# Block attention feeding a snake MLP: two batches per step, two tokens per partition, attention in one block of 64x64 tiles

## Chip, cores, metric

One core of one Trainium2 chip. The time is the device time of the core in microseconds (us), the median of several executions; a profiled execution gives a "span", about 1.9 us shorter. Lower is better. Some executions of a kernel fall into a slower state with a lower clock (the kernel before: 239.35 us at a clock of 0.986 against 234.49 us at 0.998, on one chip). Ratios and their 95% intervals use runs of the fast state alone; a median is that of all runs. The experiments' rounds ran on six different chips, so kernels of different rounds are compared by their ratios to the kernel before, which ran in every round.

The engines are PE (TensorE; PEld are its weight loads), DVE (VectorE), ACT (ScalarE), POOL (GpSimd) and SP (SyncE). Matmuls write into PSUM, which the kernels use in banks (m_ps, A_ps and Z_ps in the views before, PS in those after).

## The reference, cut to what matters

```python
# q, k, v: (4 batches, 8 heads, 768 tokens, 64), float32; block = 64
for b in range(nb):                                     # linear attention with decay lam[h]
    intra = ((qb @ kb.T) * Dmask) @ vb                  # inside the block, causal
    inter = (qb * lam_pow) @ kv_state                   # from the running state
    out[block] = intra + inter
    kv_state = lam_block * kv_state + (kb * rev_pow).T @ vb
x = out.transpose(0, 2, 1, 3).reshape(3072, 512)        # heads side by side
h = x @ w_in                                            # 512 -> 2048
g = h + sin(alpha * h) ** 2 / (alpha + 1e-9)            # "snake"
y = g @ w_out                                           # 2048 -> 512, float32 out
```

Both kernels work in tokens of 128 and six "chunks" of 512 tokens. Attention is done in 24 "steps". The scaled q and k (a power of lam each) replace the decay mask, so that the state needs no scaling.

## The kernel before

A small recorder takes operations in program order. PE keeps that order; the other engines' operations are ordered once, before the launch, by a simple simulation that uses assumed durations. Each engine then executes its queue strictly in that order (below, DVE stands 6.26 us in front of one operation with finished work queued behind it). A step is one batch, 128 tokens, all 8 heads. A load puts one token into each of 128 partitions, as 8 packets of 256 bytes. In the names, T are the transposes of q and k, S the products of k and q inside a block, O the output (`intra` and `inter` of the reference) and Z the product of k and v that updates the state. xT is the attention's output as the MLP reads it, gT the activation between the MLP's two halves; each half's weights, w_in and w_out, are loaded in blocks.

```python
def load(s):                                   # one step: three DMAs of 256 KB, on SP's queue
    b, n, r = s // NB, s % NB, s % RL
    sl = slice(n * BL, (n + 1) * BL)
    for nme, src, dst in (("k", k, k32), ("q", q, q32), ("v", v, v32)):
        a = src[b, :, sl, :].rearrange("h p d -> p h d")
        rec_load(lambda e, a=a, d=dst[r]: e.dma_start(d[:, :, :], a), ...)

def att_T(s, bank=None):                       # 8 transposes 128x128, then one copy
    for jp in range(HP):
        last = e.transpose(dst[:, jp, :], q2[c][:, 2 * jp:2 * jp + 2, :], ident[:, :])
    ...                                        # the same for k
    rec("DVE", lambda e: e.tensor_copy(qkT[j][:, :, :], dst), 0.7, ...)

def att_S(s):                                  # visit 1: S = k q^T in tiles of 64x128, then the mask
    for jp in range(HP):
        for h in range(2):
            rows = slice(64 * h, 64 * h + 64)
            last = e.matmul(A_ps[:, 4 * h + jp, :], qkT[j][rows, 4 + jp, :], qkT[j][rows, jp, :])
    ...

def att_O(s, bank=None):                       # visit 2: inter 128x128, intra 128x64, Z; then T of the next step
    ...

def grp_A(c, m):                               # MLP in: 4 matmuls 128x512 = one "group"
    ...                                        # PE -> ACT sin -> square (POOL mostly) -> DVE gT
def grp_B(c, s4, m4, bank):                    # MLP out: 4 matmuls = one group
    ...
    if m4 == 3:
        rec("ACT", lambda e: e.copy(osb[o][:, :], m_ps[bank][:, :]), 0.6, ...)
        row0 = TCH * c + 128 * s4
        rec("ACT", lambda e: e.dma_start(out[row0:row0 + 128, :], osb[o][:, :]), 0, ...)
...
for c in range(1, NCH):                        # from chunk 1 on: B of chunk c and A of chunk c + 1 alternate,
    for i in range(NM):                        # with the two attention visits of a step among 8 groups
        grp_B(c, i // 4, i % 4, bank)
        attend(4 * (c + 2), 2 * i, 8, 2, 6, 2)
        grp_A(c + 1, i)
        attend(4 * (c + 2), 2 * i + 1, 8, 2, 6, 2)
```

Of the kernel before, what the change touches and what calls it, by code (L numbers as in the profile page):

```python
# [6 lines left out]
ALU = mybir.AluOpType  # L7
# [7 lines left out]
class Op:  # L15
    __slots__ = ("eng", "fn", "deps", "dur", "idx", "sem_after", "slot", "kslot",
                 "pos", "users", "start", "end", "nbytes", "clock", "prio", "signal", "soft", "soft_users")

    def __init__(self, eng, fn, dur, idx):
        self.eng, self.fn, self.dur, self.idx = eng, fn, dur, idx  # L20
        self.deps = set()
        self.soft = ()
        self.slot = None
        self.kslot = 0
        self.signal = False
        self.prio = idx


class Program:
# [41 lines left out]
    def schedule(self, hop=0.12, rate=270e3, dma_fixed=2.0, issue=0.65):  # L71
# [10 lines left out]
        free = {e: 0.0 for e in self.ENGINES}  # L82
# [9 lines left out]
        while len(order) < n:  # L92
# [26 lines left out]
            if op.slot is not None:  # L119
                free[e] = t + issue  # L120
                dma_free = max(dma_free, t + issue) + op.nbytes / rate
                op.end = dma_free + dma_fixed
            else:
                op.end = t + op.dur
                free[e] = op.end
# [14 lines left out]
    def emit(self, nc, sem):  # L140
# [9 lines left out]
        for op in order:  # L150
            k = known[op.eng]
            need = {}
            for d in op.deps:
                if d.slot is not None:
                    key, val = ("dma", d.slot), d.kslot
                else:
                    if d.eng == op.eng and op.slot is None and d.eng == "PE":
                        continue
                    key, val = d.eng, d.pos
# [48 lines left out]
def bass_lightning_attn__then__act_snake_kernel(  # L208
# [12 lines left out]
    DM = H * D  # L221
# [8 lines left out]
    HP = H // 2  # L230
    RL = 6
    RC = 5
    NPS = 5
    RT = 4
# [4 lines left out]
    with es:  # L239
# [9 lines left out]
        q32 = ring("q32", RL, [128, H, D], F32)  # L249
        k32 = ring("k32", RL, [128, H, D], F32)  # L250
        v32 = ring("v32", RL, [128, H, D], F32)
        q2 = ring("q2", RC, [128, H, D], BF16)
        k2 = ring("k2", RC, [128, H, D], BF16)
        v2 = ring("v2", RC, [128, H, D], BF16)
        qkT = ring("qkT", 2, [128, 8, 128], BF16)
        S_m = ring("S_m", 2, [128, 8, 128], BF16)
        Zs = ring("Zs", 2, [128, HP, 128], BF16)
# [7 lines left out]
        mask = sb("mask", [128, 128], BF16)  # L265
        zeros = sb("zeros", [128, 512], BF16)
        maskf = sb("maskf", [128, 128], F32)
        ident = sb("ident", [128, 128], BF16)
        lam_bc = sb("lam_bc", [128, H], F32)
        E_i = sb("E_i", [128, NB, H], I32)  # L270
        E_f = sb("E_f", [128, NB, H], F32)
        lnlam = sb("lnlam", [128, H], F32)
        lnL = sb("lnL", [128, NB, H], F32)
        Lq = sb("Lq", [128, NB, H], F32)
        Lk = sb("Lk", [128, NB, H], F32)
# [7 lines left out]
        A_ps = es.enter_context(nc.psum_tensor("A_ps", [128, 8, 128], F32))  # L283
        Z_ps = es.enter_context(nc.psum_tensor("Z_ps", [128, HP, D], F32))
        m_ps = [es.enter_context(nc.psum_tensor(f"m_ps_{i}", [128, 512], F32)) for i in range(NPS)]
# [3 lines left out]
        nm_at = [0]  # L289
        last_load = [None]  # L290

        def rec_load(fn, writes, slot, nbytes, after=()):
            soft = (last_load[0],) if last_load[0] is not None else ()
            last_load[0] = rec("SP", fn, 0, writes=writes, slot=slot, nbytes=nbytes, after=after, soft=soft)

        def next_bank():
            i = nm_at[0] % NPS
            nm_at[0] += 1
            return i

        wblk, gate = [], {}
        last_mask = [None]

        def load(s):
            after = [gate[s]] if s in gate else []
            b, n, r = s // NB, s % NB, s % RL
            sl = slice(n * BL, (n + 1) * BL)
            for nme, src, dst in (("k", k, k32), ("q", q, q32), ("v", v, v32)):
                a = src[b, :, sl, :].rearrange("h p d -> p h d")
                rec_load(lambda e, a=a, d=dst[r]: e.dma_start(d[:, :, :], a),  # L310
                         [f"{nme}32.{r}"], f"{nme}{r}", 330000, after)

        def consts():
# [4 lines left out]
            rec("POOL", lambda e: e.iota(E_i[:, :, :], [[128, NB], [0, H]], base=0, channel_multiplier=1), 0.2,  # L318
                writes=["E_i"])
            rec("DVE", lambda e: e.tensor_copy(E_f[:, :, :], E_i[:, :, :]), 0.2, reads=["E_i"], writes=["E_f"])  # L320
            rec("ACT", lambda e: e.activation(lnlam[:, :], lam_bc[:, :], ACTF.Ln), 0.3,
                reads=["lam", "table"], writes=["lnlam"])
            ln_b = bass.AP(lnlam, 0, [[H, 128], [0, NB], [1, H]])
            rec("DVE", lambda e: e.tensor_tensor(lnL[:, :, :], E_f[:, :, :], ln_b, ALU.mult), 0.2,
                reads=["E_f", "lnlam"], writes=["lnL"])
            rec("ACT", lambda e: e.activation(Lq[:, :, :], lnL[:, :, :], ACTF.Exp), 0.3,
                reads=["lnL"], writes=["Lq"])
            rec("ACT", lambda e: e.activation(Lk[:, :, :], lnL[:, :, :], ACTF.Exp, scale=-1.0), 0.3,
# [3 lines left out]
                out=ident[:, :], in_=maskf[:, :], pattern=[[-1, 128]], compare_op=ALU.not_equal, fill=1.0,  # L332
                base=0, channel_multiplier=1), 0.3, reads=["maskf"], writes=["ident"])
            rec("POOL", lambda e: e.affine_select(
                out=mask[:, :], in_=maskf[:, :], pattern=[[-1, 128]], compare_op=ALU.is_gt, fill=1.0,
                base=0, channel_multiplier=1), 0.3, reads=["maskf"], writes=["mask"])
# [3 lines left out]
            for i in range(2):  # L340
                rec("DVE", lambda e, i=i: e.memset(Zs[i][:, :, :], 0.0), 0.3, writes=[f"Zs.{i}"])
# [3 lines left out]
        def alpha_ops():  # L345
            rec("ACT", lambda e: e.dma_start(alpha_r[:, :], moe_alpha.rearrange("(m p) -> m p", p=128)), 0,
                writes=["alpha_r"], slot="alpha", nbytes=8192)
            rec("PE", lambda e: e.transpose(Z_ps[:, 0, 0:NM], alpha_r[:, :], identf[0:NM, 0:NM]), 0.3,
                reads=["alpha_r", "identf"], writes=["Z"])
            rec("ACT", lambda e: e.copy(alpha_sb[:, :], Z_ps[:, 0, 0:NM]), 0.2, reads=["Z"], writes=["alpha"])  # L350
# [4 lines left out]
        def w_block(j, soft=(), after=()):  # L355
            if j < 4:
                cs = slice(512 * j, 512 * (j + 1))
                src = moe_w_in[:, cs].rearrange("(c p) f -> p c f", p=128)
                op = rec("POOL", lambda e: e.dma_start(w1[:, :, cs], src), 0, writes=[f"w1.{j}"],
                    slot=f"w1_{j}", nbytes=700000, soft=soft, after=after)  # L360
            else:
                j2 = j - 4
                src = moe_w_out[512 * j2:512 * (j2 + 1), :].rearrange("(m p) d -> p m d", p=128)
                op = rec("POOL", lambda e: e.dma_start(w2[:, 4 * j2:4 * (j2 + 1), :], src), 0, writes=[f"w2.{j2}"],
                    slot=f"w2_{j2}", nbytes=700000, soft=soft, after=after)
            wblk.append(op)

        def prep(s, fast=False, soft=()):
            n, r, c = s % NB, s % RL, s % RC
            Lq_b = bass.AP(Lq, n * H, [[NB * H, 128], [1, H], [0, D]])  # L370
            Lk_b = bass.AP(Lk, n * H, [[NB * H, 128], [1, H], [0, D]])
            done = rec("POOL", lambda e: e.tensor_tensor(k2[c][:, :, :], k32[r][:, :, :], Lk_b, ALU.mult), 1.05,
                       reads=[f"k32.{r}", "Lk"], writes=[f"k2.{c}"], soft=soft)
            rec("DVE" if fast else "POOL", lambda e: e.tensor_tensor(q2[c][:, :, :], q32[r][:, :, :], Lq_b, ALU.mult),
# [287 lines left out]
```

## Time and profile before

| | before |
|---|---|
| time, median (3 runs) | 234.67 us (234.05 to 237.13) |
| span of the profiled run, granted clock | 232.7 us, 1.000 |
| first MLP matmul | 22.5 us |
| first MLP matmul of chunk 1 | 64.0 us |
| end of the last MLP matmul to the end of the span | about 3 us |
| step period in the steady part | 8.59 us |

The first view is the page of the profiled execution. The rows of digits cut the span into 40 slices: each digit is the busy share in tenths, or for PEclk the clock that TensorE was granted.

```profile
span 232.7 us, 3924 instructions
PE 211.0 (91%) x1571; PEld 105.4 (45%) x1598; DVE 128.4 (55%) x169; ACT 123.2 (53%) x217; POOL 134.1 (58%) x141
...
PE   0687988697999989999999999999999999999994
...
PEclk9999999999999999999999999999999999999999
...
q1 hardware_dynamic: 74880, 18.88, 42.7%
...
q10 hardware_dynamic: 3632, 6.31, 7.4%
...
out_dram<-osb ACTq DMA_DIRECT2D x24, 256.0 KB, 2.0
```

PE is the busiest engine, and its idle time lies in the first third. q1 is SP's queue, the loads; q10 is ACT's queue, the 24 stores of 256 KB. A store lands 2.0 us after its issue. The columns of a queue are packets, megabytes, and the packets' time as a share of 16 DMA engines' span.

The second view gives stretches of the same run: the stretch, its length, busy time of each engine (with its count), the granted clock, the mean busy share of the 16 DMA engines, and GB/s.

```profile
core 0: us, PE busy (x) PEld busy (x) DVE busy (x) ACT busy (x) POOL busy (x), PEclk, DMA share, GB/s
...
4.00:9.00 5.00, 1.69 (x17) 1.29 (x17) 1.74 (x3) 2.76 (x7) 1.83 (x2) 1.00 1.29 228
...
45.00:64.00 19.00, 16.58 (x170) 9.07 (x174) 10.21 (x12) 7.77 (x16) 6.21 (x6) 1.00 1.10 222
...
86.00:216.00 130.00, 129.09 (x899) 63.27 (x913) 69.80 (x92) 72.19 (x124) 83.10 (x82) 1.00 0.34 80
216.00:233.00 17.00, 13.58 (x63) 5.96 (x61) 1.84 (x3) 3.03 (x5) 0.00 (x0) 1.00 0.20 77
```

From 4 to 9 us the loads move 228 GB/s with all DMA engines busy (a share above 1 means that the times of packets on one engine overlap). From 86 to 216 us PE is busy 129.1 of 130 us, so there only less work on PE can gain.

The third view is PE's timeline over one step of the steady part (start, duration, engine, line, operation, output<-inputs, shapes, count).

```profile
170.65 0.81 PE L470 MATMUL m_ps<-xT,w 128*128 128x512 bf16 x3
...
173.98 0.40 PE L410 MATMUL A_ps<-qkT 64*128 64x128 bf16 x8
...
177.78 0.39 PE L430 MATMUL A_ps<-qkT,Zs 128*128 128x128 bf16 x4
178.09 0.41 PE L434 MATMUL A_ps<-S_m,v_2 128*64 128x128 bf16 x8
178.34 0.29 PE L449 MATMUL Z_ps<-v_2,k_2 128*64 128x64 bf16 x8
178.56 0.40 PE L396 MATMUL A_ps<-ident,q_3 128*128 128x128 bf16 x4
178.79 0.39 PE L398 MATMUL A_ps<-ident,k_3 128*128 128x128 bf16 x4
179.23 0.81 PE L470 MATMUL m_ps<-xT,w 128*128 128x512 bf16 x3
```

The group at 170.65 and the one at 179.23 stand at the same place of two steps: the period is 8.58 us. Eight MLP groups take 8 x 0.864 = 6.91 us of it, so the two visits of attention cost about 1.68 us a step.

### The profile page before, as it was taken

To read this page: it belongs to the slowest core of one execution; us is meant where nothing else is said; L and a number is where in the kernel's file an instruction comes from. 1 tells how busy PE (TensorE), PEld (TensorE's weight loads), DVE (VectorE), ACT (ScalarE), POOL (GpSimd) and SP (SyncE) were. 2 spreads that over 40 slices of the span, in tenths; PEclk is the share of its full clock that TensorE was granted. 3 is DMA by queue.
4 is the path that set the end of the run, shared out by engine and by line. 5 is a ranking of instruction groups with operands and counts; after the bars stand their busy time and mean duration, and the time that the engine had idled before them with its cause. 6 is when DMAs were issued, how large, how long until landed. Compare 5 with 4: busy or idle time off the path is not lost.

```text
span 232.7 us, 3924 instructions
## 1 busy us (share of the span) xinstructions
PE 211.0 (91%) x1571; PEld 105.4 (45%) x1598; DVE 128.4 (55%) x169; ACT 123.2 (53%) x217; POOL 134.1 (58%) x141
## 2 busy tenths in 40 slices
PE   0687988697999989999999999999999999999994
PEld 0354433244455544455455455455455444444441
DVE  1664599745668876645636645546556535545300
ACT  4345774032787885655655655575465454454221
POOL 3253789340569897669568568758754554454100
PEclk9999999999999999999999999999999999999999
DMA  6999999999999999999670110111011011101112
GB/s 142 219 182 159 206 195 206 216 207 202 250 294 203 226 215 218 249 223 219 139 180 1 48 45 9 40 45 43 5 45 46 2 45 45 45 3 45 64 71 90
DMA packets 82752, 29.61 MB, mean 127 GB/s; under 512 B 75552, under 2 KB 79664, under 8 KB 82736
## 3 DMA queue, kind: packets, MB, share of 16 engines
q1 hardware_dynamic: 74880, 18.88, 42.7%
q0 software_dynamic: 4224, 4.19, 11.4%
q10 hardware_dynamic: 3632, 6.31, 7.4%
q8 instruction: 12, 0.20, 0.4%
q14 instruction: 4, 0.03, 0.0%
HBM read 27.28 MB, written 6.29 MB: 144 GB/s over the span
## 4 chain that ended last, share of the span: by engine, by line
PE 73%; DVE 8%; DMA 5%; SPq 4%; ACT 3%; issue 2%; POOL 2%; ACTq 0%; POOLq 0%
PE m_ps L498 33%; PE m_ps L470 28%; SPq L310 4%; DVE gT L488 3%; DMA w<-in_moe_w_out_dram 3%; PE A_ps L410 3%; DVE S_m L414 3%; PE A_ps L434 2%; DMA q_3<-in_q_dram 2%; PE A_ps L396 2%; PE A_ps L398 1%; POOL u_1 L486 1%; PE A_ps L430 1%; POOL u_0 L486 1%; ACT xT L443 1%
## 5 line engine op out<-in xcount | busy, mean ns | idle before, releaser
L498 PE MATMUL m_ps<-w,gT 128*128 128x512 bf16 x377 | 94.0, 380 | 2.7 <-DVE gT L488 1.3
L470 PE MATMUL m_ps<-xT,w 128*128 128x512 bf16 x366 | 92.3, 380 | 3.8 <-DVE gT L488 1.7
L498 PEld LDWEIGHTS m_ps<-w,gT 128*128 128x128 bf16 x384 | 36.6, 98 | 46.6 <-DVE gT L488 1.7
L470 PEld LDWEIGHTS m_ps<-xT,w 128*128 128x128 bf16 x384 | 35.2, 98 | 43.0 <-DVE gT L488 3.1
L486 POOL TENSOR_TENSOR u_0<-t_0 128x512 bf16<-128x512 bf16 x24 | 25.1, 1047 | 23.1 <-ACT t_0 L474 23.1
L414 DVE TENSOR_TENSOR S_m<-A_ps,mask 128x1024 bf16<-128x1024 f32 x24 | 29.4, 1223 | 11.7 <-PE A_ps L410 11.0
L488 DVE SCALAR_TENSOR_TENSOR gT<-u_1,r_sb,m_ps 128x512 bf16<-128x512 bf16 x24 | 17.9, 746 | 23.3 <-POOL u_1 L486 23.3
L488 DVE SCALAR_TENSOR_TENSOR gT<-u_3,r_sb,m_ps 128x512 bf16<-128x512 bf16 x24 | 17.9, 744 | 20.7 <-POOL u_3 L486 19.9
L486 POOL TENSOR_TENSOR u_1<-t_1 128x512 bf16<-128x512 bf16 x24 | 24.9, 1038 | 5.1 <-ACT t_1 L474 5.0
L486 POOL TENSOR_TENSOR u_2<-t_2 128x512 bf16<-128x512 bf16 x24 | 24.9, 1039 | 5.1 <-ACT t_2 L474 5.0
L474 ACT ACTIVATE t_2<-m_ps,alpha_sb 128x512 bf16<-128x512 f32 x24 | 16.5, 687 | 19.4 <-PE m_ps L470 19.3
L474 ACT ACTIVATE t_1<-m_ps,alpha_sb 128x512 bf16<-128x512 f32 x24 | 16.5, 687 | 18.1 <-PE m_ps L470 18.1
L486 POOL TENSOR_TENSOR u_3<-t_3 128x512 bf16<-128x512 bf16 x12 | 12.5, 1039 | 23.0 <-ACT t_3 L474 23.0
L474 ACT ACTIVATE t_0<-m_ps,alpha_sb 128x512 bf16<-128x512 f32 x24 | 16.5, 687 | 15.3 <-PE m_ps L470 15.2
L488 DVE SCALAR_TENSOR_TENSOR gT<-u_0,r_sb,m_ps 128x512 bf16<-128x512 bf16 x24 | 17.8, 740 | 10.1 <-POOL u_0 L486 10.1
L488 DVE SCALAR_TENSOR_TENSOR gT<-u_2,r_sb,m_ps 128x512 bf16<-128x512 bf16 x24 | 17.9, 744 | 9.6 <-POOL u_2 L486 9.6
L443 ACT CAST xT<-A_ps 128x512 bf16<-128x512 f32 x20 | 11.6, 582 | 20.9 <-PE A_ps L434 15.4
L506 ACT COPY osb<-m_ps 128x512 f32<-128x512 f32 x24 | 14.1, 586 | 15.6 <-PE m_ps L498 15.5
L474 ACT ACTIVATE t_3<-m_ps,alpha_sb 128x512 bf16<-128x512 f32 x24 | 16.5, 687 | 4.0 <-PE m_ps L470 3.8
L401 DVE COPY qkT<-A_ps 128x1024 bf16<-128x1024 bf16 x20 | 13.7, 684 | 4.7 <-PE A_ps L398 4.7
L457 ACT CAST Zs<-Z_ps 64x256 bf16<-64x256 f32 x40 | 14.6, 366 | 0.6
L410 PE MATMUL A_ps<-qkT 64*128 64x128 bf16 x192 | 10.0, 226 | 2.0 <-DVE qkT L401 1.9
(173 smaller groups left out, 176.8 us busy)
## 6 DMA issues: line engine op xcount, KB each, us to landing
out_dram<-osb ACTq DMA_DIRECT2D x24, 256.0 KB, 2.0
w<-in_moe_w_in_dram POOLq DMA_DIRECT2D x4, 512.0 KB, 8.0
w<-in_moe_w_out_dram POOLq DMA_DIRECT2D x4, 512.0 KB, 6.8
k_0<-in_k_dram SPq DMA_DIRECT2D x4, 256.0 KB, 4.4
q_0<-in_q_dram SPq DMA_DIRECT2D x4, 256.0 KB, 5.1
v_0<-in_v_dram SPq DMA_DIRECT2D x4, 256.0 KB, 5.4
k_1<-in_k_dram SPq DMA_DIRECT2D x4, 256.0 KB, 5.5
q_1<-in_q_dram SPq DMA_DIRECT2D x4, 256.0 KB, 5.8
```

Of the source, the lines that this page charges most:

```text
L310: rec_load(lambda e, a=a, d=dst[r]: e.dma_start(d[:, :, :], a), [f"{nme}32.{r}"], f"{nme}{r}", 330000, after)
L401: rec("DVE", lambda e: e.tensor_copy(qkT[j][:, :, :], dst), 0.7, reads=[key], writes=[f"qkT.{j}"])
L410: last = e.matmul(A_ps[:, 4 * h + jp, :], qkT[j][rows, 4 + jp, :], qkT[j][rows, jp, :])
L414: rec("DVE", lambda e: e.tensor_tensor(S_m[j][:, :, :], A_ps[:, :, :], mask_b, ALU.mult), 1.25, reads=["S0", "S1", "mask"], writes=[f"S_m. ...
L443: rec("ACT", lambda e: e.copy(xT[x][:, :, col:col + 128], dst), 0.62, reads=[key], writes=[f"x.{x}.{s % 4}"])
L457: rec("ACT", lambda e, rows=rows, cols=cols: e.copy(Zs[j][rows, :, cols], Z_ps[rows, :, :]), 0.4, reads=["Z"], writes=[f"Zs.{j}"])
L470: last = e.matmul(m_ps[i][:, :], w1[:, kc, 128 * m:128 * (m + 1)], xT[x][:, kc, :], start=(kc == 0), stop=(kc == NKC - 1))
L474: rec("ACT", lambda e: e.activation(t16[tt][:, :], m_ps[i][:, :], ACTF.Sin, scale=alpha_sb[:, m:m + 1]), 0.7, reads=[f"m.{i}", "alpha"], w ...
L486: return e.tensor_tensor(u16[tt][:, :], t16[tt][:, :], t16[tt][:, :], ALU.mult)
L488: rec("DVE", lambda e: e.scalar_tensor_tensor(out=gT[g][:, m, :], in0=u16[tt][:, :], scalar=r_sb[:, m:m + 1], in1=m_ps[i][:, :], op0=ALU.m ...
L498: last = e.matmul(m_ps[bank][:, :], gT[g][:, m, 128 * s4:128 * (s4 + 1)], w2[:, m, :], start=(m == 0), stop=(m == NM - 1))
L506: rec("ACT", lambda e: e.copy(osb[o][:, :], m_ps[bank][:, :]), 0.6, reads=[f"m.{bank}"], writes=[f"o.{o}"])
```

## The change

Its intent: make attention cheaper on PE and loads cheaper on the DMA engines. A step becomes two batches x 64 partitions, with two neighbouring tokens in each partition and four of the eight heads. A packet becomes 2 tokens x 64 x 4 bytes = 512 bytes. With 64 partitions per batch everything in attention can run in tiles of 64x64, four beside each other, so that transposes, S, intra, inter and Z of three different steps run in one visit. Around that, the order of the stages is new, the MLP's PSUM banks rotate through a list, and the loads of steps 4 to 11 are released by the third w_out block's landing. Because the tokens of a partition are neighbours, the rows that come out of the MLP are permuted, and the store has to put them back.

The core of the diff, with cuts:

```diff
-        for nme, src, dst in (("k", k, k32), ("q", q, q32), ("v", v, v32)):
-            a = src[b, :, sl, :].rearrange("h p d -> p h d")
-            rec_load(lambda e, a=a, d=dst[r]: e.dma_start(d[:, :, :], a), [f"{nme}32.{r}"], ...)
+        for nme in what:
+            for u in range(2):                       # u: which batch of the two
+                off = (((2 * pair + u) * H + HS * hh) * S + n * BL) * D
+                a = bass.AP(src.tensor, off, [[2 * D, 64], [S * D, HS], [1, 2 * D]])
+                op = rec_load(lambda e, a=a, d=dst[r], u=u: e.dma_start(d[half(u), :, :], a), ...)
 ...
-        def att_T(s, bank=None): ...
-        def att_S(s): ...
-        def att_O(s, bank=None): ...
+        def sec(t=None, o=None, s=None, tb=None, sb_=S_BK, ob=O_BK, copy_eng="DVE"):
+            # one visit: transposes of step t, output and state of step o, S of step s
+            ...
+            seqs = [block(first), block(mid), block(second)]   # each spread over four 64x64 tiles
+            ...                        # "second" waits until "first" has retired (a fence)
 ...
-                row0 = TCH * c + 128 * s4
-                rec("ACT", lambda e: e.dma_start(out[row0:row0 + 128, :], osb[o][:, :]), 0, ...)
+                row0 = (2 * pair + u) * S + n * BL
+                dst = bass.AP(out.tensor, row0 * DM, [[DM, 2], [2 * DM, 64], [1, DM]])
+                rec("ACT", lambda e: e.dma_start(dst, osb[o][:, :]), 0, ...)
 ...
-    def schedule(self, hop=0.12, rate=270e3, dma_fixed=2.0, issue=0.65):
+    def schedule(self, hop=0.1, rate=270e3, begin=1.2, done=1.2):
+        issue = {"SP": 0.25, "POOL": 0.8, "ACT": 0.5}
```

## The prediction

> **What bounds the kernel now.** The span is 232.7 us at full clock (cores view). The MLP is 768 matmuls of 128x512 at 0.216 us start to start: 166 us that stay. The chain of waits is 73% PE, with its gaps early.
>
> 1. Head: the first MLP matmul starts at 22.5 us. Until 16.6 us the chain is the load of step 3's q. Loads are 256-byte packets; the trace's take 18 ns (median) on one of 16 engines, about 220 GB/s (windows view: 218).
> 2. Chunk 1's first MLP matmul starts at 64.0 us: of the 41.5 us between, 32 MLP groups are 27.6, four attention steps about 6.6; the rest waits, mostly for the last w_out blocks (6.5 us in the chain) and the S, mask, O round trips.
> 3. Steady state, 86 to 216 us: PE is busy 129.1 of 130 us (windows). A step's period is 8.59 us (starts in the chain); 8 MLP groups are 6.91, so attention costs 1.68: streams of about 1.2 us, and gaps of about 0.1 us around its two visits and between its array shapes (timeline).
>
> **What changes.** Loads become 512-byte packets. The few in the trace take 27 ns, about 300 GB/s (estimate): 2.6 us a step instead of 3.6.[...] Weights start near 12 us instead of 16.4.
>
> Attention becomes one visit per step in 64x64 tiles: 32 transposes, 16 S, 16 intra, 8 inter, 16 Z: at 56 ns per 128 columns and four tiles in parallel, 0.90 us.[...] The trace shows column pairs 4 ns apart every 56 ns; quads it does not show. I add 0.2 for entering and leaving, 0.15 for the fence (the second part waits for the first to retire) and 0.05 for same-tile neighbours: 1.3 us instead of 1.68. On the 16 steps after chunk 1 starts that is 6 us.
>
> **The sum.** First MLP matmul at 16.5 us, partly at half clock (no warm-up matmuls); that hides behind what follows. Weights land until about 36 us. Loads of steps 4 to 7 are gated behind the third w_out block (33 us), so step 7 lands near 46 and chunk 1 starts near 51 (now 64): 13 us gained. After it: 160 MLP groups, 138 us; 17 visits of 1.3, 22; stalls 3 (four PSUM banks in rotation, POOL squares in chunk 1, xT evictions); end 2.5, as now. Span 216.5; timed runs are 1.9 above it: **218.5 us, range 211 to 226**. Faster by over 2%: 0.95; within 2%: 0.04; slower: 0.01.
>
> **What would show it.** Right: near 300 GB/s before 14 us and half the load packets (37,000); first MLP matmul at 15 to 18 us; chunk 1 at 49 to 54; step period 8.1 to 8.3 us; PE still over 97% busy there. Wrong: visits of 1.6 us or more; PE waiting for gT writes, with four banks.
>
> **What would make it wrong.** Dispatch of 176 small PE instructions per visit slower than 5 ns each; a cold PE at the start that is not hidden; DVE (about 6 of 8.2 us per step) or POOL limiting chunks 1 and 2; late loads for steps 4 to 7. The other way: visits near 1.1 us and chunk 1 at 48 would give 210.

51 + 138 + 22 + 3 + 2.5 = 216.5 us, and about 1.9 more make the 218.5. In the visit's 0.90 + 0.2 + 0.15 + 0.05 = 1.3 us, 0.90 takes the 56 ns from the trace before; four tiles in parallel were my assumption, which only the trace after shows. The 0.2 follows from the gaps of about 0.1 us before. The 0.15 and 0.05, and the 3 us of stalls, were my estimates without a measurement behind them; what was measured stands in the points at the end.

## The result, and the profile after

The changed kernel is correct and takes 279.69 us (median of 4 runs, 278.81 to 280.52). The kernel before, on the same chip in the same rounds, took 235.9 us. The ratio is 1.1887, 95% interval 1.1775 to 1.1999: it is 19% slower. A ratio here is the mean time of one kernel's fast runs over that of the other's fast runs of the same rounds, so it is not quite the ratio of the medians quoted.

| | before | predicted | after |
|---|---|---|---|
| time | 235.9 | 218.5 | 279.7 |
| span, granted clock | 232.7, 1.000 | 216.5 | 277.9, 0.931 |
| first MLP matmul | 22.5 | 16.5 | 25.6 |
| third w_out block lands | | 33 | 40.8 |
| chunk 1's first MLP matmul | 64.0 | 51 | 78.0 |
| step period, steady part | 8.59 | 8.1 to 8.3 | 8.76 |
| end of last MLP matmul to end of span | 3 | 2.5 | 16 |

The page after:

```profile
span 277.9 us, 6346 instructions
PE 215.0 (77%) x2755; PEld 107.1 (39%) x2785; DVE 131.2 (47%) x181; ACT 132.0 (48%) x212; POOL 121.8 (44%) x137
...
PE   0446999494592686978979999999999999999600
...
PEclk9999999959589599899999999999999999999975
...
q1 hardware_dynamic: 39168, 18.88, 24.1%
...
q10 hardware_dynamic: 3296, 6.30, 6.7%
...
L409 DVE TENSOR_TENSOR q<-q,Lq 128x512 bf16<-128x512 f32 x20 | 17.0, 850 | 33.1 <-DMA q<-in_q_dram 30.7
...
out_dram<-osb ACTq DMA_DIRECT2D x24, 256.0 KB
```

Four things differ. PE has two more holes, up to slice 20 and in the last two slices. The packets of the loads halved (74,880 to 39,168), as meant. The scaling of q on DVE waited 30.7 us for loads. And the store line has lost its last figure: the profile finds no moment at which a store landed. Its queue, q10, has 336 packets fewer with the same bytes. Those are packets of 4 bytes: 416 before and 80 after in the trace. I read them as completions, one for each DMA engine that worked on the DMA: on SP's queue there are 1,152 for 72 loads and 2,304 for 144, 16 for each. With the two small loads of ACT's queue, 416 is 26 x 16 and 80 is 24 x 2 + 2 x 16. **Each store of the changed kernel ran on 2 of the 16 DMA engines.**

The stretches after:

```profile
4.00:9.00 5.00, 0.90 (x33) 0.72 (x33) 1.28 (x2) 2.00 (x5) 2.35 (x3) 1.00 0.71 198
...
64.00:78.00 14.00, 7.59 (x136) 4.13 (x127) 4.14 (x6) 5.01 (x8) 6.18 (x9) 0.67 0.62 179
...
152.00:216.00 64.00, 60.85 (x822) 30.02 (x829) 38.33 (x52) 34.74 (x57) 29.72 (x32) 1.00 0.10 31
216.00:261.00 45.00, 44.79 (x206) 20.38 (x208) 14.24 (x20) 19.95 (x32) 14.58 (x14) 1.00 0.12 40
261.00:278.00 17.00, 0.82 (x4) 0.20 (x2) 0.00 (x0) 0.59 (x1) 0.00 (x0) 0.67 0.12 48
```

In the first stretch the loads move 198 GB/s, less than before, and this with the DMA engines only 0.71 busy: something other than the engines limits them. From 64 to 78 us, where PE waits for loads, the engines are 0.62 busy. In the last 17 us almost nothing works but DMA, at a share of 0.12, which is 2/16: the stores are still running off two engines. Their rate agrees: a store's packet of 2,048 bytes takes 84 ns (median), so two engines would move 49 GB/s (estimate from these two numbers); 48 were moved.

What a late load does to the rest is seen at 86 us. First DVE's timeline, then PE's, with the idle time before an instruction and what ended it in brackets.

```profile
84.14 0.74 DVE L642 SCALAR_TENSOR_TENSOR gT<-u,r_sb,PS 128x512 bf16<-128x512 bf16 x1
91.15 0.69 DVE L409 TENSOR_TENSOR q<-q,Lq 128x512 bf16<-128x512 f32 x1 [6.26 <-DMA q<-in_q_dram]
91.76 2.72 DVE L642 SCALAR_TENSOR_TENSOR gT<-u,r_sb,PS 128x512 bf16<-128x512 bf16 x4
```

```profile
84.94 1.04 PE L629 MATMUL PS<-xT,w 128*128 128x512 bf16 x4 [0.82 <-DVE gT L642]
92.56 1.89 PE L629 MATMUL PS<-xT,w 128*128 128x512 bf16 x4 [6.58 <-DVE gT L642]
```

The chain names DVE's gT write as PE's releaser, but DVE was not busy: it stood 6.26 us in front of a q scaling whose load landed at 91.13, and the gT writes were queued behind it. That load was issued at 80.59. It shares a semaphore with the load issued just before it; of the pair's 32 updates, 16 for each load, 28 had come by 83.47 and 4 came from 90.22 to 91.13. Most pairs issued from 52 to 74, 76 to 94 and 117 to 137 us show the same four late updates, 1 to 7 us behind the rest. That fits two engines which run late for both loads; the packed trace doesn't name the engine of an update. In e1_store16 below, with whole stores, no pair from 51 to 94 us shows four such updates.

The steady part, at the same place of two steps:

```profile
188.00 0.22 PE L437 MATMUL PS<-ident,q 64*64 64x64 bf16 x2
...
189.55 0.81 PE L652 MATMUL PS<-w,gT 128*128 128x512 bf16 x3 [0.16 <-issue]
...
191.06 1.03 PE L652 MATMUL PS<-w,gT 128*128 128x512 bf16 x4
192.34 1.04 PE L629 MATMUL PS<-xT,w 128*128 128x512 bf16 x4 [0.26 <-DVE gT L642]
...
196.76 0.22 PE L437 MATMUL PS<-ident,q 64*64 64x64 bf16 x2
```

Period 196.76 - 188.00 = 8.76 us. The visit, from gap to gap, takes 1.41 to 1.42 us. From 191.06 to 192.34 a group takes 1.28 us instead of 0.86: PE waits 0.42 us for a PSUM bank, once in each step. 8.76 - 6.91 - 0.43 = 1.42.

### The profile page after: what moved, and what is told of

It reads as the page before. It is cut to its first block, busy times and chain, and to the rows that moved or that the text cites. A ratio compares the mean times of both kernels' runs of the same rounds, so it can differ in the third digit from the quotient of the medians.

```text
span 277.9 us, 6346 instructions
## 1 busy us (share of the span) xinstructions
PE 215.0 (77%) x2755; PEld 107.1 (39%) x2785; DVE 131.2 (47%) x181; ACT 132.0 (48%) x212; POOL 121.8 (44%) x137
## 3 DMA queue, kind: packets, MB, share of 16 engines
q1 hardware_dynamic: 39168, 18.88, 24.1%
## 4 chain that ended last, share of the span: by engine, by line
PE 48%; DMA 14%; SPq 14%; DVE 11%; POOL 3%; issue 2%; ACT 2%; ACTq 0%; DVEq 0%
PE PS L652 20%; PE PS L629 19%; SPq L333 14%; DMA w<-in_moe_w_out_dram 7%; DMA q<-in_q_dram 5%; DVE gT L642 4%; PE PS L437 3%; DVE S_m L614 3%; PE PS L459 2%; DMA v<-in_v_dram 2%; DVE qkT L609 2%; PE PS L446 2%; POOL w L395 1%; POOL u L640 1%; DVE Zacc L587 1%
## 5 line engine op out<-in xcount | busy, mean ns | idle before, releaser
L640 POOL TENSOR_TENSOR u<-t 128x512 bf16<-128x512 bf16 x74 | 78.1, 1063 | 87.7 <-ACT t L633 87.5
L629 PE MATMUL PS<-xT,w 128*128 128x512 bf16 x375 | 97.0, 394 | 13.7 <-DVE gT L642 10.5
L652 PE MATMUL PS<-w,gT 128*128 128x512 bf16 x363 | 94.7, 395 | 4.3 <-issue 3.4
L642 DVE SCALAR_TENSOR_TENSOR gT<-u,r_sb,PS 128x512 bf16<-128x512 bf16 x96 | 69.9, 745 | 52.5 <-POOL u L640 45.9
L633 ACT ACTIVATE t<-PS,alpha_sb 128x512 bf16<-128x512 f32 x96 | 65.1, 686 | 55.0 <-PE PS L629 54.1
L629 PEld LDWEIGHTS PS<-xT,w 128*128 128x128 bf16 x384 | 37.7, 101 | 63.4 <-DVE gT L642 15.7
L652 PEld LDWEIGHTS PS<-w,gT 128*128 128x128 bf16 x384 | 37.0, 101 | 45.8 <-issue 5.7
L409 POOL TENSOR_TENSOR k<-k,Lk 128x512 bf16<-128x512 f32 x23 | 24.0, 1043 | 24.0 <-DMA k<-in_k_dram 18.6
L409 DVE TENSOR_TENSOR q<-q,Lq 128x512 bf16<-128x512 f32 x20 | 17.0, 850 | 33.1 <-DMA q<-in_q_dram 30.7
L614 DVE TENSOR_TENSOR S_m<-PS,mask 128x1024 bf16<-128x1024 f32 x24 | 29.1, 1218 | 4.8 <-PE PS L446 1.8
L418 ACT CAST v<-v 128x512 bf16<-128x512 f32 x24 | 14.9, 620 | 29.8 <-DMA v<-in_v_dram 26.5
L459 PE MATMUL PS<-S_m,v 64*64 64x128 bf16 x384 | 18.6, 248 | 10.0 <-ACT xT L596 5.9
L437 PEld LDWEIGHTS PS<-ident,q 64*64 64x64 bf16 x384 | 10.3, 116 | 23.7 <-issue 8.1
L639 ACT ACTIVATE u<-t 128x512 bf16<-128x512 bf16 x22 | 13.8, 629 | 0.6
## 6 DMA issues: line engine op xcount, KB each, us to landing
out_dram<-osb ACTq DMA_DIRECT2D x24, 256.0 KB
w<-in_moe_w_in_dram POOLq DMA_DIRECT2D x2, 256.0 KB, 6.4
```

The lines of the kernel that those rows point to most:

```text
L409: rec(eng, lambda e: e.tensor_tensor(dst[c][:, :, :], s_in, L_b, ALU.mult), 0.63 if eng == "DVE" else 1.05, reads=[f"{x}32.{r}.0", f"{x}32 ...
L418: rec("ACT", lambda e: e.copy(v2[c][:, :, :], v32[r][:, :, :].rearrange("p h (t d) -> p (h t) d", t=2)), 0.62, reads=[f"v32.{r}.0", f"v32. ...
L437: last = e.transpose(dst, src[half(u), hid(h, tt), :], ident[half(u), half(u)])
L459: return e.matmul(dst, v2[o % RC][half(u), hid(h, tj), :], S_m[o % RS][half(u), h % 2 ^ u, h // 2, tj, :], start=start, stop=True, skip_gr ...
L614: rec("DVE", lambda e: e.tensor_tensor(S_m[s % RS][:, :, :, :, :].rearrange("p r a t i -> p (r a) (t i)"), PS[:, sb_:sb_ + 2, :].rearrange ...
L629: last = e.matmul(PS[:, i, :], w1[:, kc, 128 * m:128 * (m + 1)], xT[x][:, kc, :], start=(kc == 0), stop=(kc == NKC - 1))
```

## The experiments

The theory after reading: three costs. Stores on two engines hold up both the end and the loads that queue behind them (S). Loads are slow for another reason than the packet's size (L): either the fixed time of issuing a DMA (0.62 us each on SP, 0.66 us apart, for 128 KB: 198 GB/s) or the 64 partitions that one DMA fills. The rest is the static order and the bank wait. The main rival was that the new attention, with 5,540 PE instructions instead of 3,169 (as recorded; about 30 records are missing in each trace), and its chains are slow in themselves.

Kernels that read or write wrong places are marked so; their times are valid, their outputs are not.

### 1. Stores with 16 engines; the same defect put into the kernel before

Edit of e1_store16 (all engines' orders unchanged):

```diff
-dst = bass.AP(out.tensor, row0 * DM, [[DM, 2], [2 * DM, 64], [1, DM]])
-e.dma_start(dst, osb[o][:, :])
+for t in range(2):          # two DMAs of 64 rows each
+    e.dma_start(bass.AP(out.tensor, (row0 + t) * DM, [[2 * DM, 64], [1, DM]]), osb[o][half(t), :])
```

> The changed kernel with each output store issued as two DMAs of 64 rows, so that no store has an outermost dimension of 2; the order of instructions on every engine stays. Theory S (the two-row interleaving puts every store on 2 of the 16 DMA engines, and the loads that share these two wait behind it): the time from the last matmul to the end falls from about 16 us to 3, the second halves of loads no longer land 4 to 7 us after the first halves between 52 and 95 us, the 6.6 us wait in chunk 1 goes, and the time falls from 279.7 to about 250 us. Theory L (the loads are late because of their own issue, 0.66 us per DMA; the stores cost only the tail): about 266 us, with chunk 1 starting at 78 us as before.

Edit of e4_before_store2, to the kernel before (rows land interleaved: wrong):

```diff
-e.dma_start(out[row0:row0 + 128, :], osb[o][:, :])
+e.dma_start(bass.AP(out.tensor, row0 * DM, [[DM, 2], [2 * DM, 64], [1, DM]]), osb[o][:, :])
```

> The kernel before, with only the address pattern of its stores changed to the one of the change (rows interleaved by two; the output is wrong on purpose). Theory S: stores take about 6 us or more each instead of 2, the tail grows by about 13 us, and loads between 60 and 110 us land late; 252 to 262 us. Theory L: the tail alone, about 248 us. If the pattern costs nothing by itself: 235 us.

Measured: e1_store16 256.9 us (256.0 to 258.3), ratio to before 1.0914 [1.0834, 1.0995]; e4_before_store2 261.7 us (258.66 to 264.17), ratio 1.1070 [1.0957, 1.1183]; the kernel before in these rounds 235.45. So the store's address pattern alone costs, by the ratios, 23 us in the new kernel and 25 us in the old one. The line of the stores in e1_store16 has a landing time again:

```profile
out_dram<-osb ACTq DMA_DIRECT2D x48, 128.0 KB, 2.5
```

The profiled spans differ by 23.7 us. 12.0 of it are the tail (from the end of the last MLP matmul to the end of the span 16.0 us, 4.1 us in e1_store16). The other 11.7 us were lost earlier: the same MLP-out groups start 0.6 us later at 42 us and 11.7 us later from 156 us on, with no change after that. The late updates above stand in this stretch.

What tells the three kinds of store apart is the outermost dimension of their access pattern: 128 rows in the kernel before (16 engines each, by the 416 packets), 2 tokens in the change (2 engines each, by the 80), and 64 rows in each half-store of e1_store16. There the store queue has 4,016 packets; less 3,072 of 2,048 bytes and the two small loads' 144, 800 are left, which is 50 x 16: 16 engines again. The two runs show what it costs. How other patterns are spread was not shown. I had read the pattern only for the order of its rows.

### 2. Fewer, larger loads

Edit of e2_load256: one DMA of 256 KB per tensor and batch for all 8 heads, every second step; 72 loads instead of 144. e3_both has this and the stores of e1_store16.

```diff
-a = bass.AP(src.tensor, off, [[2 * D, 64], [S * D, HS], [1, 2 * D]])
+a = bass.AP(src.tensor, off, [[2 * D, 64], [S * D, 2 * HS], [1, 2 * D]])     # only for even s
```

> The changed kernel with one load DMA of 256 KB for both steps that share a block of tokens (72 load DMAs instead of 144, the same 512-byte packets). Theory L (the issue of a load DMA takes a fixed 0.62 us on its queue, so loads of 128 KB cannot pass 200 GB/s): a DMA issues every 0.9 us or so, the rate before 14 us rises to about 290 GB/s, the last load of the first four steps lands at about 15 us instead of 20.7, the first MLP matmul comes at about 20 us instead of 25.6, and the time falls to about 262 us. Theory S: the head gains the same few us, but the loads from 50 us on stay late behind the stores; about 273 us. If the issue cost goes with the number of descriptors instead, a DMA issues every 1.24 us and nothing changes.

> Both edits. If S and L are both causes and add up: chunk 1 starts at about 58 us instead of 78, the tail is 3 us, no wait for a load over 3 us after that, and the time is about 238 us. What remains above the 218.5 predicted is then the steady part (8.76 us a step) and the cold start. If something else holds the early stages: above 248 us.

Measured: e2_load256 280.6 us, ratio 1.1906 [1.1818, 1.1993]; e3_both 256.84 us, ratio 1.0910 [1.0839, 1.0981]. Merging gains nothing (279.7 and 256.9 without it). The issue takes 0.62 to 0.64 us for 256 KB too while the queue isn't full, so it did not grow with the size here; halved in number, it no longer limits, and the loads hit the next limit. In e3_both, early:

```profile
4.00:9.00 5.00, 0.28 (x1) 0.17 (x1) 0.95 (x3) 2.00 (x5) 1.60 (x2) 1.00 1.21 225
```

The engines are now busy all the time and move only 225 GB/s. A 512-byte packet takes 44 ns (median) where in the changed kernel it took 27 to 29, and one load of 256 KB completes per 1.19 us. What still differs from a fast load is that it fills 64 partitions.

### 3. The same loads into 128 partitions

Theory H, here and in experiment 4, is that filling only 64 partitions limits the rate.

Edit of e8_load128, to e3_both; same packets, bytes and number of DMAs, but the data are wrong:

```diff
-off = ((2 * pair + u) * H * S + n * BL) * D
-a = bass.AP(src.tensor, off, [[2 * D, 64], [S * D, 2 * HS], [1, 2 * D]])     # into d[half(u), :, :]
+off = ((2 * pair * H + HS * u) * S + min(n * BL, 512)) * D
+a = bass.AP(src.tensor, off, [[2 * D, 128], [S * D, HS], [1, 2 * D]])        # into d[:, HS*u:HS*u+HS, :]
```

> The kernel with both edits; each load DMA keeps its 256 KB, its count and its 512-byte packets, but fills all 128 partitions of half of a tile (256 tokens of one batch and four heads) instead of 64 partitions of the whole tile. The data are wrong on purpose; the order on PE, DVE, ACT and POOL is the same. Theory H[...]: packets take about 27 to 30 ns instead of 44, one load lands every 0.87 us instead of 1.19, the last load of the first four steps lands at about 14.5 us instead of 18.3, and the rate from 4 to 9 us is 290 to 300 GB/s. Rival R (512-byte packets in a full queue are limited elsewhere): 44 ns and 1.19 us as before. If H holds, this run also tells what the load rate is worth: chunk 1 should start at about 66 us instead of 75, and the time be about 247 us instead of 256.8; if chunk 1 stays near 75, the order of work and not the rate holds it.

Measured: 246.66 us (245.87 to 247.21), ratio 1.0523 [1.0478, 1.0569]. That is 10.2 us below e3_both by the medians, which are of two chips, and about 9 us by the ratios.

```profile
4.00:9.00 5.00, 0.28 (x1) 0.18 (x1) 1.65 (x3) 2.21 (x6) 2.50 (x2) 1.00 1.09 288
```

In this stretch a packet takes 27 ns again and the rate is 288 GB/s, near the 300 of the prediction. The last load of the first four steps lands at 14.96 us (18.31 in e3_both). So the 512 bytes do bring what was predicted, but only into 128 partitions.

The runs show that the same packets are faster into 128 partitions (27 against 44 ns and 288 against 225 GB/s, from 4 to 9 us); by which mechanism was not shown. One rival isn't excluded by this run alone: e8_load128 also reads four heads of 128 row pairs per DMA instead of eight heads of 64, another order of reading on the HBM's side. Experiment 4 leaves that side as it was.

### 4. Filling both halves through two queues

Edit of e5_two_queues, to e3_both: the loads of the second batch (partitions 64 to 127) of the first four steps are issued on ACT's queue.

> The kernel with both edits (stores of 64 rows, loads of 256 KB); for the first four steps the loads of the second batch of a pair, which fill the upper 64 partitions, are issued from ACT's queue, so that both partition halves are written at once. Theory H[...]: packets of 512 bytes take about 27 to 30 ns again instead of 44, the rate from 4 to 9 us rises from 225 to 290 GB/s or more, and the last load of the four steps lands at about 14 us instead of 18.3. Rival R (two-token packets are limited on the HBM side or by the queue as a whole): the rate stays within 210 to 235 GB/s and the last load lands at 18 us.

Measured (one run, state unknown): 259.06 us. The loads do get faster in the second half of the stretch,

```profile
9.00:14.00 5.00, 0.00 (x0) 0.00 (x0) 1.33 (x2) 0.00 (x0) 2.60 (x2) 1.00 1.21 270
```

from 219 GB/s in e3_both to 270, and the last one lands at 16.66 us. But alpha's small load queued behind them on ACT and landed at 16.8 us. PE's first instruction needs alpha and started at 16.87, with all of PE's work behind it, which put the first MLP matmul at 28.8 us. A miss in time; it shows that two DMAs that fill different halves overlap in part: +5% (236 against 225 GB/s) from 4 to 9 us and +23% from 9 to 14 us.

e9_combo used both queues for 12 steps, with alpha first, measured durations in the scheduler and an earlier release of the loads.

> An attempt at a version that beats both kernels: both edits, the copies on ACT, the second batch's loads on ACT's queue for the first twelve steps, the scheduler's durations as measured, loads of steps 4 and later gated by the second w_out block instead of the third, weights issued behind k and q instead of behind v, and a few warm-up matmuls before the first MLP matmul. If the causes found so far add up: first MLP matmul at about 21 us, chunk 1 at about 63 us, steady period 8.33 us, and 238 to 242 us. Below 230 us would mean that the change's attention visits pay once its data movement is mended; above 248 us that the stage order itself costs more than its data movement.

Measured: 267.52 us, ratio 1.1385 [1.1277, 1.1493] (its profiled run was slow, the ratio uses fast ones; what follows is read from the slow one). It failed: ACT, which has sin, copies and stores to do, stood in front of its own loads (1.6 to 2.2 us for each issue while the queue was full, longer for the release), and PE waited once 14.9 us for gT. The queue on a busy engine was not free here.

### 5. The bank wait

In the changed kernel DVE has gT, the state sum (0.42 us), the qkT copy (0.68 us) and the mask (1.22 us) in each step. Edit of e6_qkt_act, to e3_both: `def steady(i, eng="DVE")` becomes `eng="ACT"`, which moves the qkT copies of the steady part to ACT.

> The kernel with both edits; in the steady part the copies of the transposed q and k go to ACT instead of DVE. Theory B (with three banks in rotation, the MLP group that needs a bank waits for a gT write that stands behind the accumulation, the copy and the mask on DVE): the wait of 0.42 us per step vanishes, a step's period falls from 8.76 to about 8.34 us, and the time falls from 256.8 to about 252 us. If the banks themselves are the limit (sin, square and gT in a row), the period stays over 8.6 us.

Measured: 253.7 us (253.36 to 256.36), ratio 1.0863 [1.0744, 1.0983]. The period falls from 8.76 to 8.33 us, the wait of 0.43 us is gone, as expected. The start of two visits in its trace:

```profile
174.62 0.22 PE L440 MATMUL PS<-ident,q 64*64 64x64 bf16 x2
...
182.94 0.22 PE L440 MATMUL PS<-ident,q 64*64 64x64 bf16 x2
```

8.33 - 6.91 = 1.42 us is the visit. Eight such steps would give 3.4 us. The medians, of two chips, differ by 3.1 us and the ratios by 1.1 us; the intervals are too wide to say more than that they don't contradict it.

### 6. The scheduler's model

The changed kernel's simulation assumed 0.25 us to issue a load and 1.2 us before its data move. Edit of e7_model, to e3_both: 0.65 and 1.9 us, and 330,000 instead of 235,000 assumed bytes for each load.

> The kernel with both edits; only the durations that the kernel's own list scheduler assumes for loads are set to the measured ones (a load DMA issues every 0.65 us and moves 256 KB in 1.22 us, starting 1.9 us after its issue), which changes the order of instructions on DVE, ACT and POOL, and nothing else. Theory M (the order is fixed for loads that come earlier than they do, so that a prep which waits for a load blocks finished work queued behind it): chunk 1 starts at about 67 us instead of 75, and the time falls to about 247 us. If the late loads themselves are the limit in any order: within 2 us of 256.8.

Measured: 255.16 us, ratio 1.0876 [1.0790, 1.0962], chunk 1 at 73.3 us, not 67. Mostly a miss: chunk 1 starts 2.0 us earlier than in e3_both (75.3), and the time gains 1.7 us by the medians, of two chips, and 0.8 us by the ratios, which is within the noise.

### 7. Squares, and the release of the loads

e10_squares is e6_qkt_act with more of chunk 1's squares on ACT (`m % 3 == 2` instead of `m % 5 == 4`) and two q scalings on DVE instead of POOL.

> This is the kernel with whole stores, 256 KB loads and the qkT copies on ACT, plus: in chunk 1 every third square on ACT instead of every fifth, and the q scaling of steps 9 and 10 on DVE instead of POOL. In its parent PE waits 1.8 to 2.8 us near the eighth visit for a gT write whose square had queued on POOL behind the q scaling. If POOL's backlog causes that wait, it goes and the time falls from 253.7 to about 252 (range 251 to 253). If DVE or the loads cause it, the wait moves to another instruction and the time stays at 253 to 255.

Measured: 258.02 us, ratio 1.0952 [1.0808, 1.1097]. The theory falls: PE still waits 2.35 us for gT before the eighth visit. The last MLP-in group of chunk 1 holds a bank that the visit needs, and from that group's end the way sin, square, gT takes about 3 us, whichever engine squares.

e11_gate is e10_squares with the model of e7_model and the loads of steps 4 on released by the first w_out block, not the third. e15_gate_only is the same without the squares.

> As the squares kernel, plus the scheduler's load times as measured, and the loads of steps 4 to 7 released by the first w_out block's landing instead of the third's. If chunk 1 is late because those loads are released late, they land about 5 us earlier, chunk 1 starts near 70 us instead of 75, and the time is about 247 (range 244 to 250). If the total of bytes at 225 GB/s decides, the w_out blocks are pushed back by as much as the loads gain, chunk 0's second half waits for them, and the time stays within 250 to 253. Neither account expects it below 235, the time of the kernel before.

> The correct kernel with whole stores, 256 KB loads, qkT copies on ACT, the scheduler's load times as measured and the loads of steps 4 to 7 released by the first w_out block, but the squares of chunk 1 as in the change. If the squares cost what their own run showed, this is 2 to 3 us better than the version with them: 247 to 249 us. If the squares' run was slower because of its chip's clock alone, this is the same as with them, 250 to 251.

Measured: e11_gate 250.46 us, ratio 1.0618 [1.0496, 1.0740]; e15_gate_only 250.43 us, ratio 1.0601 [1.0411, 1.0791]. So these two runs show no effect of the squares. Chunk 1 starts at 69.1 and 69.0 us instead of 75.0. The loads themselves land hardly earlier (step 4's last q at 46.66 instead of 46.82 us), which fits their sharing the DMA engines with the w_out blocks; which of the two edits gave the 6 us was not separated, but e7_model, with the model's edit alone, had started chunk 1 only 2.0 us earlier. It is the best correct version of the change together with e17_warm below, and still 6% slower than the kernel before. No version beat it.

### 8. Everything at once (wrong)

e12_all_wrong is e8_load128 with the edits of e6 and e10, and of e11 the release by the first w_out block and the 1.9 us of the model; the model's time of issue and its bytes stay as they were.

> The output is wrong on purpose: load DMAs fill 128 partitions each, as in the earlier run of that kind (246.7 us), and all that was found since is in it too: qkT copies on ACT, more squares on ACT in chunk 1, loads released by the first w_out block, and the scheduler's fixed time of a load raised. If the causes found[...] are all there is, their gains nearly add: 246.7 less 3 for the copies, 1.5 for the squares, 3 to 5 for the gate, so 237 to 240 us, the step period near 8.35 and chunk 1 near 61. If the rest is dominated by the static order of chunk 0's second half and PE's fetch stalls, it stays at 242 to 246.

Measured: 246.31 us, ratio 1.0437 [1.0296, 1.0579]; chunk 1 at 67.2 us (its profiled run was slow, at 248.62 us). A miss: the gains of the causes found till then (stores, half-filled loads, bank waits, POOL's backlog, release) do not add; the interval holds e8_load128's 1.0523. Fast loads that were released earlier did not land earlier, which fits their sharing the DMA engines with the weights (step 4's last q lands at 43.75 us in that slow run; 42.54 us in e8_load128).

### 9. Late loads, or round trips?

In e8_load128 the last load of steps 4 to 7 lands at 49.7 us, near the 46 of the prediction, but chunk 1 starts at 65.3 us, not at 51. e14_no_loads was to leave these loads out and let their scalings read the data of steps 0 to 3.

> The output is wrong on purpose. The kernel with 128-partition loads (246.7 us, chunk 1 at 65.3), where steps 4 to 7 are not loaded at all: their scalings read the data of steps 0 to 3 that is there. If late loads make chunk 1 late, PE no longer waits 4 us for step 4, the second half of chunk 0 takes 22 to 24 us instead of 30, chunk 1 starts at 57 to 59, and the time is 238 to 241. If the round trips between PE and the copies, in PE's fixed order, make it late, only the 4 us wait goes: chunk 1 at 61 to 63 and 242 to 244 us. If nothing of it is the loads, it stays at 65 and 246.

Measured: 247.34 us, ratio 1.0456 [1.0153, 1.0760], chunk 1 at 66.3 us. It was my mistake and says nothing: the loads of steps 8 to 11 are recorded earlier than those scalings and went into the same buffers, so that the scalings waited for them (43.24 us). e16_loads_there records the loads of steps 8 to 11 after the scalings of steps 5 and 7.

```diff
-if hh:
+if hh or 4 <= s < 8:                                  # no loads of steps 4 to 7
     return last_load[0]
-r, c = (s // 2) % RL2, s % RC
+r, c = (s // 2 - 2 * (4 <= s < 8)) % RL2, s % RC      # their scalings read steps 0 to 3
-if s >= 8: load_next()
+for _ in range(1 if s >= 8 else 2 if s in (5, 7) else 0): load_next()
```

> The output is wrong on purpose. As the run without the loads of steps 4 to 7 (247.3 us, chunk 1 at 66.3), and the loads of steps 8 to 11 are now recorded after the scalings of steps 5 and 7, so that the scalings of steps 4 to 7 wait for no load at all. If late loads make chunk 1 late, PE does not wait before step 4's transposes, the second half of chunk 0 takes 22 to 25 us instead of 30, chunk 1 starts at 57 to 60, and the time is 238 to 242. If the round trips between PE and the copies, in PE's fixed order, make it late, only the 4 us wait goes: chunk 1 at 61 to 63 and 242 to 244.

PE in e8_load128, and then in e16_loads_there, at the first visit of chunk 0's second half:

```profile
43.57 0.42 PE L440 MATMUL PS<-ident,q 64*64 64x64 bf16 x8 [4.36 <-DVE q L412]
```

```profile
38.76 4.48 PE L655 MATMUL PS<-w,gT 128*128 128x512 bf16 x20
43.17 0.32 PE L440 MATMUL PS<-ident,q 64*64 64x64 bf16 x8
```

Measured: 245.08 us, ratio 1.0478 [1.0393, 1.0562]. The wait is gone and this half of chunk 0, from its first MLP-out matmul to chunk 1, takes 25.3 us instead of 30.6, so 5.3 us of it were loads. Chunk 1 still starts at 64.2 us, because another order of the scalings at the head made the first MLP matmul 2.7 us and chunk 0's first half 1.3 us later. Of the 25.3 us, 13.8 are MLP groups and about 7 are visits; the rest is waits, the longest 2.55 us for an xT copy on ACT before the last visit. Neither theory alone: of the 9.7 us that this half of chunk 0 takes in e8_load128 beyond its groups and visits, 5.3 are loads, and the rest stands in the row of visits behind them in PE's fixed order.

### 10. Stops with nothing to wait for

Inside visits PE sometimes stops for 0.5 to 2.8 us with no semaphore. In e6_qkt_act three such stops came at PE's instructions 1473, 2241 and 2753, all 193 modulo 256: 768 and 512 instructions apart. That instructions are fetched in blocks of 256 was at this point a theory which fits these distances. e13_fetch_shift puts 50 tiny matmuls (100 instructions) before PE's first transpose.

> The kernel with whole stores, 256 KB loads and qkT copies on ACT, with 50 tiny matmuls (100 PE instructions) put in front of PE's first transpose, in time that PE is idle. In its parent PE stops with nothing to wait for before its instructions 1473, 2241 and 2753 (193 modulo 256), 1.7 us at the last, inside the visit of chunk 1's end. If PE's instruction fetch in blocks of 256 causes the stops, the instruction numbers stay (193 modulo 256), so that the stops hit work that stands 100 instructions earlier in the program than before. If the work itself or the time on the clock causes them, they stay with the same work, at 2853. The time stays within 2 us of 253.7.

Measured in one run, state unknown: 248.91 us; the count of its instructions has gaps (29 of 5,692 records missing), and there the stops come at about 705, 1468 and 2485, so near 193 modulo 256, at work that is not that of before. e17_warm puts the same 50 matmuls into e15_gate_only.

> The correct gate-only version (250.4 us, clock 0.972) with the 50 tiny matmuls in front of PE's first transpose. If PE's low granted clock between 42 and 92 us, where it idles, comes from work too sparse early on and those matmuls mend it, the granted clock is 0.99 or more and the time falls to 245 to 247. If the shifted kernel's 5 us were the chance of one run or of another order, it stays at 249 to 251.

Measured: 249.27 us (248.05 to 249.70), ratio 1.0617 [1.0559, 1.0676], granted clock of the profiled run 0.983. By the ratios (1.0617, and 1.0601 for e15_gate_only) the warm matmuls gain nothing here, so the 5 us of the shifted run, which was not repeated, are not put down to them. But its trace is complete (5,692), and the stops stand at instructions 449, 705 and 1217: again 193 modulo 256, although everything is shifted by 100. One of them:

```profile
55.05 0.22 PE L449 MATMUL PS<-qkT 64*64 64x128 bf16 x2
57.24 0.22 PE L485 MATMUL PS<-v,k 64*64 64x64 bf16 x2 [1.96 <-issue]
```

The number stays and the work changes, so it is the instruction stream, not the work. The profile has a queue of the kind "instruction" (q8). It moved 0.36 MB in the changed kernel and 0.20 MB before, as 22 and 12 packets of 16 KB, one for about 252 and 264 of the 5,540 and 3,169 PE instructions; so I take a packet for a block of 256. The landings bear it out: in e17_warm such packets landed at 17.20, 23.97 and 55.54 us, and the three stops ended 1.2, 1.4 and 1.7 us later. The stops of e6_qkt_act, e7_model and e1_store16 at such numbers end 1.3 to 1.6 us after a landing, and in these traces no instruction at such a number starts sooner than 1.2 us after its block's landing. So in these stops PE waits for its next block of instructions. Once the loads have ended (at 112 us in e17_warm), the blocks land at least 3.4 us ahead. With the old order of PE (e4_before_store2, a complete trace) they land at least 9.8 us ahead all along. The kernel before has two stops of 0.41 us, one at instruction 705, also 193 modulo 256; its block had landed 16.7 us earlier, so that stop is of another kind. A few stops stand at other numbers (1.37 us near instruction 1049 of e5_two_queues, 0.56 us near 1249 of e3_both) and stay unexplained. The stops that follow a landing stand where PE spends 176 instructions in a visit of 1.4 us while loads are running.

## Why the prediction was wrong, point by point

- **The bound of the kernel before** was read rightly (MLP on PE in the steady part, late loads in front), and the two tables above rest on the same readings.
- **"end 2.5, as now"** is the step that failed most. The prediction took the stores for unchanged; their address pattern put them on 2 engines. The tail was 16 us, and the loads behind the stores added as much again before: 23 us in all (experiment 1).
- **"Loads become 512-byte packets ... about 300 GB/s"** is the second failed step. Packets were halved as said, but the changed kernel moved 198 GB/s, limited by 0.62 us of issue for each of twice as many DMAs, and after merging 225 GB/s into 64 partitions. With 128 partitions it was 288. The prediction measured 512-byte packets in the trace of before on other loads, and did not ask into how many partitions the new ones go. Worth about 9 us by the ratios (experiment 3). So the weights started at 17.3 us, not 12, the third w_out block landed at 40.8, not 33, and everything gated behind it followed.
- **"step 7 lands near 46 and chunk 1 starts near 51"**: even with fast loads (49.7 us) chunk 1 came at 65.3. The prediction gave 5 us to work that took 15: six visits and more than ten MLP groups stand in PE's order behind step 4's load. 5.3 us of it go with the loads (experiment 9), the rest stays. The head was mis-sized too: first MLP matmul at 20.9 us in e8_load128, 6 us after its last load, where the prediction had 16.5.
- **"Visits 1.3 us instead of 1.68"**: the assumption was right and the size a little off: 1.42 us. Quads do run in parallel: in the trace four starts fall within 20 ns, again and again every 56 ns. The terms were first and middle part 0.5 us, gap of the fence 0.2, second part 0.5, entering and leaving 0.2 (whole gaps of about 0.1 us on entering and 0.1 to 0.16 us on leaving).
- **"stalls 3"** was mis-sized. "PE waiting for gT writes, with four banks" was named as a sign of being wrong, and it came: 0.43 us in each step, which turns the gain of 0.26 us of a visit into a period 0.17 us longer (8.76 against 8.59). In e8_load128, where stores and loads are cured, chunk 1's start to the end takes 178.3 us against 168.7 before and 165.5 predicted. PE's timeline shows six waits of 0.8 to 2.5 us in chunks 1 and 2, 6.9 us together: gT and xT waits, and a stop of 0.9 us of the kind of experiment 10.
- **The granted clock** fell to 0.67 where PE idled (64 to 78 us, PE busy 7.59 of 14). The prediction had a cold PE only at the head. There it came as said: about the first dozen MLP matmuls start 0.427 us apart instead of 0.216. In the kernel before, which has 11 warm-up matmuls of 128x512 from 9.2 to 21.8 us, they start 0.215 us apart from the first on; e17_warm's tiny matmuls did not prevent it (again about a dozen at 0.427). That the missing warm-up causes it was not shown by a run of its own. What the clock alone costs was not separated.

What remains open: how much each of the waits in chunks 1 and 2 costs by itself, and how the 6 us of e15_gate_only divide between its two edits. In sum, of the 44 us that the changed kernel loses to the kernel before, by the ratios 23 are the stores, about 9 the half-filled loads, and about 12 remain when both are mended. These 12 are put down to the new waits of the attention part, in chunk 0 and after, and to the lower clock. That is read from PE's timeline; no run that removes them all shows it. Against them the shorter visit gains about 0.26 us a step.

## What to carry to other kernels

When a change permutes the data, look at both ends of it before counting packets: at each DMA's outermost dimension (here 2 went with 2 of the 16 engines and cost 23 us, 64 and 128 went with 16) and at how many partitions it fills (here, with the queue full, a 512-byte packet took 44 ns into 64 and 27 ns into 128). A landing time that vanishes from the profile, or a DMA share that stands at 2/16 while everything waits, was here the mark of a DMA that sat on few engines. And where queues are in order and the order is fixed beforehand, an operation that waits for a late load holds back finished work behind it (here DVE's q scaling for 6.26 us): read which instruction an idle engine stands in front of, not only which engine the chain names.
